# All pairs of a linear-attention kernel: k's sums and numerators in plain float32, two heads side by side in 64-column tiles, sums of k and denominators in four 32-column tiles

## The chip, the cores and the metric

The kernel runs on one core of a Trainium2 chip. TensorE (PE) multiplies matrices, VectorE (DVE) and ScalarE (ACT) work on tiles, GpSimd (POOL) makes one reduction, and SyncE (SP) starts the DMA transfers. The metric is the device time of one launch in microseconds (us), the median of several runs. The profiled execution is one more run, with its own time.

## The reference

The inputs are `q`, `k`, `v` of 8 batches, 8 heads, 576 positions and 64 numbers a head, `w_phi` (64 x 128) and three weights of a gated layer. Cut to what matters:

```
proj = x @ w_phi                                  # for q and for k: 576 x 128 a head
proj = proj - max(abs(proj), axis=-1)
phi  = concat(exp(proj), exp(-proj))              # 576 x 256
kv   = phi(k).T @ v                               # 256 x 64 a head
z    = phi(k).sum(over positions)                 # 256
num  = phi(q) @ kv ;  den = phi(q) @ z + 1e-6
x    = num / den, heads side by side              # 4608 tokens x 512
out  = ((x @ w_a) * (x @ w_b)) @ w_out            # 512 -> 1536 -> 512
```

All of it is float32.

## The kernel before, in words

**Products.** TensorE reads float32 in two ways here. A tile of type `F32` is multiplied as plain float32, where one matmul of the program shows as two records in the trace. A tile of type `F32R` is a rounded form that takes one record, and a float32 value is kept as two of these, a high part and a low part (`split`, lines 154 to 157: a cast, and a subtraction that finds the low part). The product of two split values is three matmuls (`products`, lines 108 to 112): high by high, high by low, low by high.

**Attention** goes by pairs of heads: 8 batches with 4 pairs, 32 pairs in all, which the text numbers 0 to 31. For a pair, `k_load` brings in k and v, `features` (lines 216 to 246) projects k in chunks of 128 positions, finds the maximum, subtracts it and takes the two exponentials. `kv_add` (lines 275 to 289) multiplies a chunk's features with v and adds into the PSUM tile `kvps`; v carries a 65th column of ones, so row 65 of the result is z. There are four full chunks (two to a `k_chunks`) and 64 positions left over, which two pairs share in one tile (`rest_chunk`, `rest_add`). `k_finish` (lines 295 to 314) copies `kvps` out, transposes it on TensorE into `pt`, and copies that to `kvh`. `kvps` and `pt` share one PSUM bank from batch 1 on (`spare`, line 293), so a pair's `kvps` waits until the readers of the `pt` before it are done. `q_project` projects q for both heads. `q_side` (lines 342 to 375) takes the maximum over partitions on GpSimd, subtracts, takes the exponentials and multiplies with `kvh`, for numerator and denominator in one, 65 rows of `pn`. `reciprocals` turns the denominators into factors.

**Which pairs are split.** The first pairs are plain float32: k's projections and q's up to pair 4, the products of `kv_add` up to pair 6 (`PLAIN_KV = 7`), the numerators up to pair 4 (`PLAIN_NUM = 5`). These five have a form of their own (`numerators`, lines 377 to 406): two heads write to rows 0 to 63 and 64 to 127 of one `pn`, each with 64 columns of weights, and the denominators go to four strips of 32 rows of `pd`. All later pairs are split: `keh`, `kel` (features of k), `vaug`, `vl` (v), `kvh`, `kvl` and `qeh`, `qel` (features of q).

**The gated layer** takes 512 tokens a block (`moe_block`, lines 618 to 671) for the first third of the 1536 columns, all in split form, while attention is still going; two later passes follow with another algorithm. `attention_steps` (lines 418 to 455) writes the stages of the pairs to turns, five turns a pair for the first seven and then four. In each turn the main loop (lines 1029 to 1040) lets `PACE` steps of the gated layer go (0.6 until turn 18, then 0.62). The order in which all this is written sets priorities; a scheduler with a model of the chip makes the final order of each engine's queue, and each engine then works through its queue in order. The places that the prediction speaks of are `kv_add`, `k_finish`, the end of `q_side`, `numerators`, and the matmuls of lines 645 and 666, the gated layer's.

## Time and profile before

| | |
|---|---|
| median of 3 runs | 1240.53 us (1240.15 to 1241.73) |
| profiled execution | 1247.55 us, span 1245.8 us |
| PE busy | 1200.6 us, 96% of the span |
| DVE busy | 1033.0 us, 83% |
| ACT busy | 696.2 us, 56% |
| POOL busy | 151.5 us, 12% |

The span is what the profiler saw from first to last instruction. A record of a matmul has a modelled end: matmuls overlap in the pipeline, so the time from one start to the next is what a matmul costs, and a busy PE can hold short gaps. POOL works until about 590 us, which is where attention ends. What follows is the rest of the first pass, and from about 700 us the later passes, which the change does not touch. In rows, `128*65` after the names is rows and columns of the weights, and `128x256` is the operand that streams past them.

### The profile page before, as it was taken

Reading aid. Unit: us, or ns where it says so; the run is one execution under the profiler, and the core shown is the slowest. Engines: PE = TensorE matmul, PEld = TensorE weight load, DVE = VectorE, ACT = ScalarE, POOL = GpSimd, SP = SyncE. Lnnn points to the kernel's source line nnn. Section 1 sums busy time; section 2 is a strip of 40 time slices with the busy share of each in tenths; the row PEclk is TensorE's granted clock in tenths of the full one; section 3 lists DMA queues with packets and bytes.
Section 4 is the critical chain, followed back from the end, with each engine's and each line's share of the span. In section 5 each row is a group of like instructions: output and inputs, shape, how many; then the busy total and the mean of one; then the engine's idle time right before and its main releaser. Section 6 shows DMA issues by size and latency. Waiting matters only on the chain.

```text
span 1245.8 us, 18250 instructions
## 1 busy us (share of the span) xinstructions
PE 1200.6 (96%) x6425; PEld 977.0 (78%) x6425; DVE 1033.0 (83%) x1742; ACT 696.2 (56%) x1317; POOL 151.5 (12%) x68
## 2 busy tenths in 40 slices
PE   7898999999999999999899999999999999999998
PEld 4456878778888878888678888888888888887887
DVE  6999988989989899796398865888888688888686
ACT  5667768778777777677244443444434243434332
POOL 2233132222231322212000000000000000000000
PEclk9999999999999999999999999999999999999999
DMA  6664443443443543323373331657489724242412
GB/s 198 186 199 119 109 136 94 118 150 102 129 127 93 145 110 113 110 80 91 93 254 102 110 97 56 211 178 241 150 279 395 262 60 153 68 149 70 129 67 86
DMA packets 125360, 174.86 MB, mean 140 GB/s; under 512 B 34571, under 2 KB 63647, under 8 KB 125269
## 3 DMA queue, kind: packets, MB, share of 16 engines
q1 hardware_dynamic: 125268, 173.71, 45.0%
q8 instruction: 50, 0.82, 0.3%
q14 instruction: 42, 0.34, 0.1%
HBM read 115.10 MB, written 58.56 MB: 139 GB/s over the span
## 4 chain that ended last, share of the span: by engine, by line
PE 47%; DVE 14%; DMA 7%; issue 2%; ACT 2%; SPq 1%; DVEq 0%; ACTq 0%
PE pba L740 6%; PE po L952 6%; PE paa L740 6%; PE po L666 4%; PE pa L645 3%; PE poa L845 3%; PE pac L740 3%; PE pb L645 3%; PE pbc L740 3%; PE kvps L282 2%; PE pn L371 2%; PE pab L740 2%; PE pbb L740 2%; DMA rb<-rec 2%; DMA x<-xnorm 1%
## 5 line engine op out<-in xcount | busy, mean ns | idle before, releaser
L348 POOL PARTITION_ALL_REDUCE mb<-p x64 | 151.4, 2393 | 433.4 <-ACT p L339 363.8
L157 DVE TENSOR_TENSOR qel<-qe,qeh 128x1152 fp32r<-128x1152 f32 x54 | 74.6, 1381 | 7.4 <-ACT qeh L150 7.4
L238 ACT ACTIVATE ke<-kd 128x512 f32<-128x512 f32 x64 | 40.5, 634 | 65.8 <-DVE kd L230 65.5
L645 PE MATMUL pb<-xh,w_b_h 128*128 128x512 f32 x144 | 59.4, 412 | 7.1 <-DVE h L650 5.5
L352 ACT ACTIVATE qe<-p 128x576 f32<-128x576 f32 x64 | 44.0, 687 | 37.6 <-DVE p L349 35.6
L157 DVE TENSOR_TENSOR kel<-ke,keh 128x1024 fp32r<-128x1024 f32 x50 | 62.1, 1242 | 3.2 <-ACT keh L150 3.1
L282 PE MATMUL kvps<-keh,vaug 128*65 128x256 f32 x200 | 56.3, 281 | 7.2 <-DVE kvl L312 7.2
L150 ACT CAST qeh<-qe 128x1152 fp32r<-128x1152 f32 x54 | 62.8, 1163 | 0.0
L666 PE MATMUL po<-hh,w_o_h 128*128 128x512 f32 x144 | 58.5, 412 | 1.9 <-DVE h L650 1.9
L645 PE MATMUL pa<-xh,w_a_h 128*128 128x512 f32 x144 | 57.9, 402 | 1.5 <-DVE xh L152 1.4
L602 DVE TENSOR_TENSOR x<-x,rb 128x512 f32<-128x512 f32 x36 | 31.9, 887 | 33.1 <-DMA rb<-rec 31.0
L666 PE MATMUL po<-hl,w_o_h 128*128 128x512 f32 x144 | 58.4, 405 | 0.3 <-DVE hl L157 0.3
L645 PE MATMUL pb<-xl,w_b_h 128*128 128x512 f32 x144 | 58.3, 405 | 0.0
L645 PE MATMUL pb<-xh,w_b_l 128*128 128x512 f32 x144 | 58.2, 404 | 0.0
L645 PE MATMUL pa<-xl,w_a_h 128*128 128x512 f32 x144 | 57.5, 399 | 0.5 <-DVE xl L157 0.5
L645 PE MATMUL pa<-xh,w_a_l 128*128 128x512 f32 x144 | 57.8, 401 | 0.0
L666 PE MATMUL po<-hh,w_o_l 128*128 128x512 f32 x144 | 57.6, 400 | 0.0
L952 PE MATMUL po<-hl,w_o_h 128*128 128x512 f32 x144 | 56.4, 392 | 0.2
L952 PE MATMUL po<-hh,w_o_l 128*128 128x512 f32 x144 | 56.1, 389 | 0.0
L282 PE MATMUL kvps<-keh,vl 128*64 128x256 f32 x200 | 55.9, 279 | 0.0
L282 PE MATMUL kvps<-kel,vaug 128*65 128x256 f32 x200 | 55.8, 279 | 0.0
L150 ACT CAST keh<-ke 128x1024 fp32r<-128x1024 f32 x50 | 52.5, 1051 | 1.8 <-PE kvps L282 1.5
(343 smaller groups left out, 3838.9 us busy)
## 6 DMA issues: line engine op xcount, KB each, us to landing
x<-xnorm SPq DMA_DIRECT2D x32, 512.0 KB
o<-part SPq DMA_DIRECT2D x61, 256.0 KB
q<-in_qT SPq DMA_DIRECT2D x32, 288.0 KB
xnorm<-x SPq DMA_DIRECT2D x36, 256.0 KB
part<-o SPq DMA_DIRECT2D x18, 512.0 KB
part<-o SPq DMA_DIRECT2D x36, 256.0 KB
k<-in_km SPq DMA_DIRECT2D x32, 256.0 KB
v<-in_vm SPq DMA_DIRECT2D x32, 256.0 KB
```

The lines of the kernel that those rows point to most:

```text
L150: eng.copy(dst, src)
L157: eng_lo.tensor_tensor(lo, src, hi, op=ALU.subtract)
L238: nc.scalar.activation(e[:, :, 0, :], d, AF.Exp)
L282: nc.tensor.matmul(st["kv_ps", b, pr][:width, j], v_[:, j, :width], e_[:, j], start=(left == NFULL and j == 0 and n_ == 0), stop=(left == ...
L348: nc.gpsimd.partition_all_reduce(mb, p32, P, bass_isa.ReduceOp.absmax)
L352: nc.scalar.activation(e[:, 0], p32, AF.Exp)
L602: nc.vector.tensor_tensor(x32, x32, rb, op=ALU.mult)
L645: nc.tensor.matmul(acc, w[:, cc * P : (cc + 1) * P], x, start=(k == 0), stop=(k == 3 * NCC - 1))
L666: nc.tensor.matmul(acc, w[:, cc * P : (cc + 1) * P], h, start=(k == 0), stop=(k == 3 * NFS[p] - 1))
L740: nc.tensor.matmul(accs[to][i], w_, x_, skip_group_check=True, **at)
L845: nc.tensor.matmul(accs[to][m], w_, x_, skip_group_check=True, **flags)
L952: nc.tensor.matmul(acc[key], w[:, cc * P : (cc + 1) * P], h[:, tok], skip_group_check=True, **n_)
```

## The change

All pairs now use the plain form for the sums of k and for the numerators; the projections stay as they were (plain up to pair 4, split after).

* `kv_add` takes the chunks of a `k_chunks` together. For each, the two heads' products with v go to rows 0 to 63 and 64 to 127 of the first half of `kvps` (64 columns of weights each, plain float32). z no longer comes from a column of ones in v: a weight tile `ones` (32 columns) multiplies each chunk and head, into four strips of 32 rows of the second half of `kvps`. For the 64 positions left over it is the same with two products and two strips.
* `k_finish` makes two transposes of 128 columns instead of four of 65, and two small products with `pick`, which adds the strips up to the two z. `kvh` stays float32, and `kvl` is gone.
* `q_side` ends with the exponentials; `numerators` does what it did for the first five pairs, for all.
* The casts and subtractions for v, for the features of k and of q, and for `kvh` are gone, and the tiles for them. Their room goes to more buffers for the plain features (`qe` 4, `ke2` 4) and for v (3), and the decoding of the weights has tiles of its own (`w`) instead of sharing `kel2`.
* A pair's two `q_side` start two turns apart instead of three, and the numerators of both heads stand at turn 12 of a pair; before, they stood at 10 and 13 (split) or 13 (plain). `PACE` is 0.68 instead of 0.62.

```diff
-Q_TURNS, Q_STEP, QB, PB, Q32 = (4, 6, 10), 3, 1, 2, 2
+Q_TURNS, Q_STEP, NUM_TURN, QB, PB, Q32 = (4, 6), 2, 12, 1, 2, 2
-PACE0, PACE, PACE0_UNTIL = 0.6, 0.62, 18
-PLAIN_K, PLAIN_Q, PLAIN_KV, PLAIN_NUM = 5, 5, 7, 5
+PACE0, PACE, PACE0_UNTIL = 0.6, 0.68, 18
+PLAIN_K, PLAIN_Q = 5, 5
...
+        ones = a1.tile([P, P // 4], F32, name="ones")
+        nc.vector.memset(ones, 1.0)
+        pick = a1.tile([P, 2], F32, name="pick")
+        nc.vector.memset(pick, 0.0)
+        for g in range(4):
+            nc.vector.memset(pick[g * P // 4 : g * P // 4 + 1, g % 2 : g % 2 + 1], 1.0)
...
-        if i >= PLAIN_KV:
-            va = vaug[pr % 2]
-            vl = a1.tile([P, NFULL, 2, D + 1], F32R, tag="vl", bufs=2, name=f"vl_{u}")
-            split(va[:, :, :, :D], vl[:, :, :, :D], v32, engine("v_hi", b), engine("v_lo", b))
-            st["v", b, pr] = (va, vl)
...
+        e = a2.tile([P, 2 * n, 2, F], F32, tag=f"ke{n}", bufs=(2, 4)[n - 1], name=f"ke_{u}")
         nc.scalar.activation(e[:, :, 0, :], d, AF.Exp)
         nc.scalar.activation(e[:, :, 1, :], d, AF.Exp, scale=-1.0)
-        es = (e,)
-        if not plain:
-            eh = a2.tile(shape, F32R, tag=f"keh{n}", bufs=n, name=f"keh_{u}")
-            el = a2.tile(shape, F32R, tag=f"kel{n}", bufs=n, name=f"kel_{u}")
-            split(eh, el, e, engine("ke_hi", i // NPAIR), nc.vector)
-            es = (eh, el)
-        yield es
+        yield e
...
-    def kv_add(b, pr, vs, es, st):
-
-        left = st["kv_left", b, pr] = st["kv_left", b, pr] - 1
-        for j in range(2):
-            parts = products(vs, es)
-            for n_, (v_, e_) in enumerate(parts):
-                width = D if n_ == 2 else D + 1
-                nc.tensor.matmul(
-                    st["kv_ps", b, pr][:width, j],
-                    v_[:, j, :width],
-                    e_[:, j],
-                    start=(left == NFULL and j == 0 and n_ == 0),
-                    stop=(left == 0 and n_ == len(parts) - 1),
-                    skip_group_check=True,
-                )
+    def kv_add(b, pr, chunks, consts, st, rows=slice(0, P)):
+
+        ones = consts[6]
+        kv = st["kv_ps", b, pr]
+        first = st["kv_left", b, pr] == NFULL + 1
+        left = st["kv_left", b, pr] = st["kv_left", b, pr] - len(chunks)
+        for c, (v, e) in enumerate(chunks):
+            at = dict(start=(first and c == 0), stop=(left == 0), skip_group_check=True)
+            for j in range(2):
+                nc.tensor.matmul(kv[j * D : (j + 1) * D, 0], v[:, j], e[:, j], **at)
+        q = P // 4
+        for c, (v, e) in enumerate(chunks):
+            for j in range(2):
+                g = 2 * c + j
+                to = kv[g * q : (g + 1) * q, 1]
+                at = dict(start=False, stop=(left == 0), skip_group_check=True)
+                nc.tensor.matmul(to, ones[rows], e[:, j], tile_position=(rows.start, g * q), **at)
...
-        kvT = a2.tile([P, 4, F], F32, tag="kb", bufs=1, name=f"kvT_{u}")
-        nc.scalar.copy(kvT[: D + 1], st["kv_ps", b, pr][: D + 1].rearrange("p j (s f) -> p (j s) f", s=2))
+        kvT = a2.tile([P, 2, 2, F], F32, tag="kb", bufs=1, name=f"kvT_{u}")
+        nc.scalar.copy(kvT, st["kv_ps", b, pr].rearrange("p k (s f) -> p k s f", s=2))
...
-        for g in range(4):
-            nc.tensor.transpose(pt[:, g, : D + 1], kvT[: D + 1, g, :], ident[: D + 1, : D + 1])
...
+        for s in range(2):
+            nc.tensor.transpose(pt[:, s, :P], kvT[:, 0, s], ident)
+        for s in range(2):
+            nc.tensor.matmul(pt[:, s, P : P + 2], kvT[:, 1, s], consts[7], skip_group_check=True)
+        kvh = a2.tile([P, 2, P + 2], F32, tag="kvh", name=f"kvh_{u}")
+        nc.scalar.copy(kvh, pt[:, :, : P + 2])
...
-            split(eh, el, e, engine("qe_hi", b), nc.vector)
...
-        for i in range(2):
-            tok = slice(i * HALF, (i + 1) * HALF)
-            pn = ps.tile([P, 512], F32, tag="att", name=f"pn_{u}_{i}")
-            for n_, (s, kv_, e_) in enumerate(parts):
-                at = dict(start=(n_ == 0), stop=(n_ == len(parts) - 1))
-                nc.tensor.matmul(pn[: D + 1, :HALF], kv_[:, 2 * j + s, :], e_[:, s, tok], **at)
-            nc.scalar.copy(xn[: D + 1, tok], pn[: D + 1, :HALF])
-        nc.sync.dma_start(xun[b][h * D : (h + 1) * D], xn[:D])
-        nc.sync.dma_start(den[b][h : h + 1], xn[D : D + 1])
```

Three places in the order of the queues show what moves. The first is TensorE at the sums of k, pair 1 of batch 4: `kvps` is the sum, `keh`, `kel`, `vaug`, `vl` the split operands, `po` the gated layer's. Before, from the end of a `po` through the first of two chunks:

```order
L666 MATMUL po_0_2_0_3869<-hl_0_2_2_3691,w_0_2_o_h_641 128x512
L666 MATMUL po_0_2_0_3869<-hh_0_2_2_3690,w_0_2_o_l_642 128x512
L282 MATMUL kvps_4_1_3848<-keh_4_1_0_3714,vaug1_131 65x256
L282 MATMUL kvps_4_1_3848<-kel_4_1_0_3715,vaug1_131 65x256
L282 MATMUL kvps_4_1_3848<-keh_4_1_0_3714,vl_4_1_3449 64x256
```

The three `kvps` rows then stand three times more. With the change, the end of the k projection `pk`, the first two chunks, the end of the `po` behind them, the other two chunks and the rest, with `ke` the plain features and `v32`, `rv32` the plain v:

```order
L200 MATMUL pk_4_1_r_3438<-wkh_110,rkl_4_1_3296 128x256
L247 MATMUL kvps_4_1_3408<-ke_4_1_0_3266,v32_4_1_2853 64x256 x4
L254 MATMUL kvps_4_1_3408<-ke_4_1_0_3266,ones_129 32x256 x4
...
L604 MATMUL po_0_2_1_3449<-hh_0_2_3_3332,w_0_3_o_l_716 128x512
L247 MATMUL kvps_4_1_3408<-ke_4_1_2_3417,v32_4_1_2853 64x256 x4
L254 MATMUL kvps_4_1_3408<-ke_4_1_2_3417,ones_129 32x256 x4
L247 MATMUL kvps_4_1_3408<-ke_4_0_r_3195,rv32_4_0_2678 64x256 x2
L254 MATMUL kvps_4_1_3408<-ke_4_0_r_3195,ones_129 32x256 x2
```

Twelve matmuls of a `k_chunks` are now eight, and the width of the weights alternates between 64, 32 and the 128 of the neighbours. The second place is TensorE at the numerators `pn` and denominators `pd` of the same pair. Before, for the first of its two heads (`qeh_4_2`), whose partner stands elsewhere in the queue:

```order
L371 MATMUL pn_4_2_0_4114<-qeh_4_2_3905,kvh_4_1_4019 65x288 x2
L371 MATMUL pn_4_2_0_4114<-qel_4_2_3906,kvh_4_1_4019 65x288 x2
L371 MATMUL pn_4_2_0_4114<-qeh_4_2_3905,kvl_4_1_4021 65x288 x2
L371 MATMUL pn_4_2_1_4122<-qeh_4_2_3905,kvh_4_1_4019 65x288 x2
L371 MATMUL pn_4_2_1_4122<-qel_4_2_3906,kvh_4_1_4019 65x288 x2
L371 MATMUL pn_4_2_1_4122<-qeh_4_2_3905,kvl_4_1_4021 65x288 x2
```

With the change, for both heads (`qe_4_2` and `qe_4_3`), from the second half of the tokens on, between a small product `pt` with `pick` and the next k projection:

```order
L272 MATMUL pt_4_2_3720<-pick_131,kvT_4_2_3650 128x2
L329 MATMUL pn_4_1_1_3696<-qe_4_2_3420,kvh_4_1_3566 64x288
L329 MATMUL pn_4_1_1_3696<-qe_4_3_3568,kvh_4_1_3566 64x288
...
L339 MATMUL pd_4_1_3702<-qe_4_2_3420,kvh_4_1_3566 32x288 x2
L339 MATMUL pd_4_1_3702<-qe_4_3_3568,kvh_4_1_3566 32x288 x2
...
L200 MATMUL pk_5_0_0_3734<-wkh_110,kh_5_0_3637 128x256
```

Both heads stand together, and the denominators are matmuls of their own. The third place is ScalarE between two exponentials of k (`ke`) of the same pair. Before:

```order
L238 ACTIVATE ke_4_1_0_3711<-kd_4_1_0_3506 128x4x128
L239 ACTIVATE ke_4_1_0_3711<-kd_4_1_0_3506 128x4x128
...
L150 CAST keh_4_1_0_3714<-ke_4_1_0_3711 128x1024
L372 COPY xn_3_6_3614<-pn_3_6_0_3615 65x288
L372 COPY xn_3_6_3614<-pn_3_6_1_3623 65x288
L150 CAST qeh_4_0_3642<-qe_4_0_3639 128x1152
L150 CAST vaug0_129<-v32_4_2_3454 128x8x64
```

With the change:

```order
L207 ACTIVATE ke_4_1_0_3266<-kd_4_1_0_3133 128x4x128
L208 ACTIVATE ke_4_1_0_3266<-kd_4_1_0_3133 128x4x128
L312 ACTIVATE qe_4_1_3374<-p32_4_0_1_3060 128x576
L313 ACTIVATE qe_4_1_3374<-p32_4_0_1_3060 128x576
L147 CAST hh_0_2_1_3179<-h32_0_2_1_3176 128x512
L207 ACTIVATE ke_4_1_2_3417<-kd_4_1_2_3241 128x4x128
```

The casts `keh`, `qeh` and `vaug` are gone from between the exponentials. On VectorE the subtractions that went with them, `kel`, `qel`, `vl` and `kvl`, are gone in the same way.

More of the change, by code (lines that the diff above doesn't have):

```diff
@@ L137, in attention_consts @@
         nc.sync.dma_start(ident, diagonal[: P * P].rearrange("(p n) -> p n", n=P))
-        vaug = []
-        for i in range(2):
-            t = a1.tile([P, NFULL, 2, D + 1], F32R, name=f"vaug{i}")
-            nc.vector.memset(t[:, :, :, D : D + 1].bitcast(F32), 1.0)
-            vaug.append(t)
-        return w2, wh, wl, wk32, (wkh, wkl), ident, vaug
+        ones = a1.tile([P, P // 4], F32, name="ones")
[4 more added lines that the diff above has]
+            nc.vector.memset(pick[g * P // 4 : g * P // 4 + 1, g % 2 : g % 2 + 1], 1.0)
+        return w2, wh, wl, wk32, (wkh, wkl), ident, ones, pick
     def engine(step, b):
@@ L197, in rest_load @@
         nc.sync.dma_start(k32, kr[b, g])
-        v32 = a1.tile([P, 2, D + 1], F32, tag="rv32", name=f"rv32_{u}")
-        nc.vector.memset(v32[:, :, D : D + 1], 1.0)
-        nc.sync.dma_start(v32[:, :, :D], vr[b, g])
+        v32 = a1.tile([P, 2, D], F32, tag="rv32", bufs=2, name=f"rv32_{u}")
+        nc.sync.dma_start(v32, vr[b, g])
+        st["rv", b, g] = v32
         yield
@@ L206, in rest_load @@
             st["rk", b, g] = (kh, kl)
-        yield
-        st["rv", b, g] = (v32,)
-        if i >= PLAIN_KV:
-            vh = a1.tile([P, 2, D + 1], F32R, tag="rvh", name=f"rvh_{u}")
-            vl = a1.tile([P, 2, D + 1], F32R, tag="rvl", name=f"rvl_{u}")
-            split(vh, vl, v32, engine("v_hi", b), engine("v_lo", b))
-            st["rv", b, g] = (vh, vl)
         yield
@@ L252, in k_chunks @@
         yield next(gen)
-        es = next(gen)
+        e = next(gen)
         yield
@@ L258, in k_chunks @@
             st["kv_left", b, pr] = NFULL + 1
-        for c in range(2):
-            kv_add(b, pr, [v_[:, c0 + c] for v_ in st["v", b, pr]], [e_[:, 2 * c : 2 * c + 2] for e_ in es], st)
+        v = st["v", b, pr]
+        kv_add(b, pr, [(v[:, c0 + c], e[:, 2 * c : 2 * c + 2]) for c in range(2)], consts, st)
         yield
@@ L298, in k_finish @@
         assert st["kv_left", b, pr] == 0
-        kvT = a2.tile([P, 4, F], F32, tag="kb", bufs=1, name=f"kvT_{u}")
-        nc.scalar.copy(kvT[: D + 1], st["kv_ps", b, pr][: D + 1].rearrange("p j (s f) -> p (j s) f", s=2))
+        kvT = a2.tile([P, 2, 2, F], F32, tag="kb", bufs=1, name=f"kvT_{u}")
+        nc.scalar.copy(kvT, st["kv_ps", b, pr].rearrange("p k (s f) -> p k s f", s=2))
         yield
         pool, tag, bufs = spare(b, ps)
-        pt = pool.tile([P, 4, P], F32, tag=tag, bufs=bufs, name=f"pt_{u}")
-        for g in range(4):
-            nc.tensor.transpose(pt[:, g, : D + 1], kvT[: D + 1, g, :], ident[: D + 1, : D + 1])
-        plain = b * NPAIR + pr < PLAIN_NUM
-        kvh = a2.tile([P, 4, D + 1], F32 if plain else F32R, tag="kvh", name=f"kvh_{u}")
-        nc.scalar.copy(kvh, pt[:, :, : D + 1])
-        st["kv", b, pr] = (kvh,)
-        if not plain:
-            kvl = a2.tile([P, 4, D + 1], F32R, tag="kvl", name=f"kvl_{u}")
-            nc.vector.tensor_tensor(kvl, pt[:, :, : D + 1], kvh, op=ALU.subtract)
-            st["kv", b, pr] = (kvh, kvl)
+        pt = pool.tile([P, 2, 2 * P], F32, tag=tag, bufs=bufs, name=f"pt_{u}")
+        for s in range(2):
[4 more added lines that the diff above has]
+        nc.scalar.copy(kvh, pt[:, :, : P + 2])
+        st["kv", b, pr] = kvh
         yield
@@ L342, in q_side @@
     def q_side(b, pr, j, a1, a2, ps, consts, st):
[L343 to L345 removed]
+        u = f"{b}_{2 * pr + j}"
         p32 = st["p", b, pr][j]
@@ L350, in q_side @@
         yield
[L351 removed]
+        e = a2.tile([P, 2, S], F32, tag="qe", bufs=4, name=f"qe_{u}")
         nc.scalar.activation(e[:, 0], p32, AF.Exp)
         nc.scalar.activation(e[:, 1], p32, AF.Exp, scale=-1.0)
[L354 to L374 removed]
+        st["qe", b, pr, j] = e
         yield
     def numerators(b, pr, a1, a2, ps, consts, st):
[L379 to L380 removed]
         u = f"{b}_{pr}"
[L382 removed]
+        kv, es = st["kv", b, pr], [st["qe", b, pr, j] for j in range(2)]
         toks = [slice(i * HALF, (i + 1) * HALF) for i in range(2)]
@@ L387, in numerators @@
             for s in range(2):
-                for j, e in enumerate((e0, e1)):
+                for j, e in enumerate(es):
                     at = dict(start=(s == 0), stop=(s == 1), skip_group_check=True)
-                    nc.tensor.matmul(pn[j * D : (j + 1) * D, :HALF], kv[:, 2 * j + s, :D], e[:, s, tok], **at)
+                    rows = slice(j * D, (j + 1) * D)
+                    nc.tensor.matmul(pn[rows, :HALF], kv[:, s, rows], e[:, s, tok], **at)
             nc.scalar.copy(xn[:, tok], pn[:, :HALF])
@@ L577, in stage @@
                 return xpool.tile(shape, dt, tag="o", bufs=2, name=name)
-            return pool.tile([P, 2 * DM], dt, tag="kel2", bufs=2, name=name)
+            return pool.tile([P, 2 * DM], dt, tag="w", bufs=2, name=name)
         return stage
```

67 lines of the change are left out of this document (14 added, 53 removed).

## The prediction

> **What bounds the kernel now.** I read the shares of busy time first, then a table by stage, then the timeline of single matmuls, and last the waits. The page and the stage table (columns: window, its length, busy time of PE, PEld, DVE, ACT, POOL, granted clock, DMA share, GB/s):
>
> ```profile
> PE 1200.6 (96%) x6425; PEld 977.0 (78%) x6425; DVE 1033.0 (83%) x1742; ACT 696.2 (56%) x1317; POOL 151.5 (12%) x68
> ```
>
> ```profile
> 31.00:124.00 93.00, 83.76 (x490) 50.70 (x487) 88.14 (x160) 66.70 (x140) 29.36 (x12) 0.98 0.56 169
> 124.00:590.00 466.00, 452.18 (x2846) 380.36 (x2845) 410.63 (x628) 350.85 (x671) 113.30 (x48) 1.00 0.40 114
> 590.00:651.00 61.00, 55.44 (x244) 43.41 (x243) 38.26 (x81) 24.09 (x50) 0.00 (x0) 0.94 0.56 170
> 651.00:1246.00 595.00, 585.16 (x2755) 487.79 (x2753) 474.57 (x826) 238.71 (x426) 0.00 (x0) 1.00 0.46 151
> ```
>
> PE is the bound in every stage but the second, where DVE is busy 88 of 93 us and PE waits for it. In 124 to 590, where the split pairs run, DVE is at 88% and PE at 97%: PE is the bound and DVE makes it wait now and then. So the change has to be judged in PE time first, and the relief of DVE and ACT counts only as far as PE waits for them. A matmul's true price is the distance between starts, since its modelled end overlaps the next:
>
> ```profile
> 302.40 0.28 PE L282 MATMUL kvps<-keh,vaug 128*65 128x256 f32 x1
> ...
> 303.68 0.28 PE L282 MATMUL kvps<-keh,vl 128*64 128x256 f32 x1
> 303.89 0.40 PE L337 MATMUL pq<-qh,wh 64*128 64x288 f32 x2
> 304.13 0.29 PE L337 MATMUL pq<-ql,wh 64*128 64x288 f32 x2
> ...
> 304.65 0.29 PE L337 MATMUL pq<-qh,wl 64*128 64x288 f32 x2
> 304.87 0.50 PE L645 MATMUL pa<-xh,w_a_h 128*128 128x512 f32 x1
> 305.21 0.39 PE L645 MATMUL pa<-xl,w_a_h 128*128 128x512 f32 x1
> 305.44 0.40 PE L645 MATMUL pa<-xh,w_a_l 128*128 128x512 f32 x1
> ...
> 308.24 0.41 PE L305 MATMUL pt<-ident,kvT 65*128 65x65 f32 x4
> 308.46 0.37 PE L226 MATMUL pk<-wkl,kh 128*128 128x256 f32 x1
> ...
> 311.60 0.42 PE L371 MATMUL pn<-qeh,kvh 128*65 128x288 f32 x2
> ...
> 313.17 0.40 PE L666 MATMUL po<-hh,w_o_h 128*128 128x512 f32 x1
> ```
>
> Eleven steps of split `kvps` take 1.28 us, **0.117 us** each. The twelve split `pn` of one head take 1.57 us, **0.131** each. Four transposes take 0.22, 0.06 each. And there is a price that no group shows: where the shape of the weights changes from 128 rows to 64 (`kvps` to `pq`) the step is 0.21 instead of 0.117, and the first `pq` takes 0.24 instead of 0.13; back to 128 rows 0.22 instead of 0.13, and the first `pa` 0.34 instead of 0.23. **One change of shape costs about 0.09 us, and 0.11 more for the first weights of 128 columns, 0.20 in all.**
>
> The plain forms that the change spreads are in the trace too, in the first pairs:
>
> ```profile
> 11.86 1.94 PE L282 MATMUL kvps<-ke,v 128*65 128x256 f32 x8
> 13.73 0.75 PE L337 MATMUL pq<-q,w 64*128 64x288 f32 x2
> ...
> 64.16 1.18 PE L399 MATMUL pd<-qe,kvh 128*32 128x288 f32 x16 [0.21 <-ACT xn L391]
> 65.26 0.75 PE L337 MATMUL pq<-q,w 64*128 64x288 f32 x2
> ...
> 73.22 0.28 PE L226 MATMUL pk<-wkh,kl 128*128 128x256 f32 x1
> 73.42 2.16 PE L390 MATMUL pn<-qe,kvh 128*64 128x288 f32 x16
> 75.52 1.16 PE L399 MATMUL pd<-qe,kvh 128*32 128x288 f32 x10
> ```
>
> A plain product shows as two records. Four plain `kvps`, one after the other, take 1.87 us to the next start, of which 0.14 is the change of shape: 0.43 each, more than three split ones (0.35). Eight plain `pn` with two heads side by side take 2.10: without 0.14 for the changes that is 0.49 for two of them, so **two heads in 64-column tiles really run at once**. Eight `pd` in four strips take 1.10, without 0.11 again 0.49 for four. For 256 elements instead of 288 that is 0.43 for two products, or four strips. Entering `pn` from `pk` costs 0.20 instead of 0.117, the 0.09 again. For narrower weights the second part of a change is smaller: 0.05 for 64 columns and 0.02 for 32, worked out from these sums.
>
> **The change part by part, on PE.** How many of each there are is counted in the order.
>
> Sums of k: before, 744 split matmuls at 0.117 and 72 plain at 0.43, 118.1 us. After, 128 times two products at once, 64 sets of four strips, and for the rest 32 times two products and 32 times two strips, each 0.43, with a few that the order tears apart: 112.3. Numerators: before 648 at 0.131 and five plain pairs, 99.9. After, six times 0.485 a pair, and some `pn` alone where gated-layer matmuls stand between the heads: 96.2. Transposes: before 128 at 0.06, 7.8. After, 64 of twice the width, for which I take 0.07, and 128 records of the small products with `pick` at 0.06 (nothing in the trace is as short; between 0.03 and 0.12): 12.3. The q projections keep their number, but the order sets two heads side by side more often: 35.3 to 29.8. Together 261.1 to 250.6, **10.5 us less**.
>
> Changes of shape: the order has 202 before and **432** after (into 64, into 32, into the next wide shape, where before a split sum or numerator stood between wide neighbours at no charge). At 0.20, 0.14 and 0.11 by the width they go into, 39.0 become 66.4, **27.4 more**. PE's own work grows by **17 us**. Bounds: 10, if only the 0.09 is paid for each of the 230, and 27, if none of the 10.5 comes in.
>
> On this the Trainium skill has a rule, in "TensorEngine Tiling (Array Packing)", Key Properties: changing the tiling mode, not just the tile, drains the engine. It speaks against this change, and the trace agrees that such a change costs. If the drain were the whole modelled tail of a record (0.28 less 0.117, 0.16) instead of the 0.09 of the rows, the 230 would cost 16 us more; the rows decide for 0.09.
>
> **What DVE and ACT give back.** In 124 to 590 the groups that go (count, busy us, mean ns, idle before):
>
> ```profile
> L157 DVE TENSOR_TENSOR qel<-qe,qeh 128x1152 fp32r<-128x1152 f32 x49 | 67.1, 1370 | 7.4 <-ACT qeh L150 7.4
> L157 DVE TENSOR_TENSOR kel<-ke,keh 128x1024 fp32r<-128x1024 f32 x49 | 60.9, 1243 | 3.2 <-ACT keh L150 3.1
> L157 DVE TENSOR_TENSOR vl<-v,vaug 128x512 fp32r<-128x512 f32 x23 | 19.8, 860 | 0.0
> L312 DVE TENSOR_TENSOR kvl<-pt,kvh 128x260 fp32r<-128x260 f32 x24 | 10.0, 416 | 0.0
> L150 ACT CAST qeh<-qe 128x1152 fp32r<-128x1152 f32 x48 | 55.8, 1162 | 0.0
> L150 ACT CAST keh<-ke 128x1024 fp32r<-128x1024 f32 x48 | 50.4, 1050 | 1.8 <-PE kvps L282 1.5
> L150 ACT CAST vaug<-v 128x512 fp32r<-128x512 f32 x23 | 14.2, 617 | 1.8 <-PE kvps L282 1.8
> ```
>
> DVE loses 158 of 411 us and falls to 54%, ACT 120 of 351, to 50%. All of it lies beside PE work, so it is worth only PE's waits. These are, by the waits of PE and one place in the timeline:
>
> ```profile
> PE kvps L282 <- DVE kvl L312: 7.2, 9, 2.1
> PE pb L645 <- DVE h L650: 5.5, 3, 2.9
> PE po L666 <- DVE h L650: 1.9, 1, 1.9
> ```
>
> ```profile
> 615.63 0.80 PE L645 MATMUL pb<-xh,w_b_h 128*128 128x512 f32 x1 [2.93 <-DVE h L650]
> 616.22 0.63 PE L645 MATMUL pb<-xl,w_b_h 128*128 128x512 f32 x1
> ```
>
> By the stage table PE is idle 9.2, 13.8 and 5.6 us in the three stages up to 651. A wait hides 0.16 us in the modelled tail before it, and behind a long one the clock is low for a while (the step at 616 is 0.43 instead of 0.23; the table's 0.98 and 0.94 are 1.9 and 3.7 us). From start to start, without the changes of shape, I count 13, 26 and 10 us in these stages, **49 in all**. What returns: in the split stage 15 of 26, since `kvps` no longer waits for `kvl`, and half-empty queues bring `h` and the features sooner; in 31 to 124 only 4 of 13, since plain pairs and the decoding of weights still fill DVE there; after 590 4 of 10, since both orders end attention with the same two and a half blocks of the gated layer or a little less. **23 in all.** Bounds: 7 (the one wait that disappears by name), and 42.
>
> `PACE` and the new turns only reorder work that PE must do anyway; their price is in the waits. A pair's four output transfers become two, and POOL is busy 24% in 124 to 590; PE waits for neither in that stage.
>
> **The sum:** 17 less 23 is **6 us less** against the profiled execution's 1247.55. That one lies 7.0 above the median 1240.53, so the median would be 1234.5; I say 1235.
>
> **The rivals.** (1) *Nearly all waits go.* With DVE and ACT at half, PE could run as in 651 to 1246, where it is idle 9.8 of 595 us, end and transitions included. For it: ample slack on every other engine. Against it: in that stage DVE is at 80% and still gives few waits, so load alone does not make them, and 31 to 124 stays full. 17 less 41: 1217. (2) *The changes of shape win.* PE pays its 17 us surely, at every pair, while the waits are those of chains that the change leaves: `pb` waits for `h`, which needs `pa` copied by ACT and multiplied by DVE with two banks between; `kvps` now waits for the copy `kvh` on ACT in place of `kvl`. It decides as soon as fewer than 17 of the 49 come back. With the 7 of the named wait alone: 10 more, 1250. For it: the rows of 0.20 are firm; against it: 8 us of the listed waits are at DVE's `h`, behind a queue that is emptied by a third. (3) *The heads do not run at once in the sums* (the change doesn't do what it says): 160 double steps and the strips one after the other, 0.43 each, add about 70 and 90 us, some 1390. Against it stand the `pn` and `pd` rows, of the same form.
>
> **How the numbers follow.** Forecast, between 15 less and 2 more: 0.50. Nearly all waits go: 0.17. Shapes win: 0.28. No overlap: 0.05. A measurement of this kernel tells about 0.2%, 2.5 us, from no change. Faster by more: 0.37 of the forecast and all of (1), 0.54. Within: 0.13 of the forecast and 0.04 of (2), 0.17. Slower: 0.24 and 0.05, 0.29. The range leaves out (3) and the ends of (1) and (2): 1219 to 1253.
>
> **What would show it.** Right: plain `kvps` groups of about 1.0 (two chunks' products) and 0.54 us (strips), steps of 0.20 around them, DVE at 55% in the attention stage, PE's listed waits below half, the later passes unchanged. Wrong: changes of shape dearer or cheaper than 0.20, or new waits of `kvps`, `pn` or `pt` on ACT's copies of the size of the old ones.

## The result: 1.3% slower

| | before | changed |
|---|---|---|
| median of four runs each | 1241.13 us (1240.15 to 1245.71) | 1258.39 us (1253.47 to 1260.68) |
| profiled execution | 1247.55 us | 1259.20 us |
| first matmul of the later passes starts at | 702.8 us | 711.8 us |

The ratio is 1.0126, with a 95% interval of 1.0087 to 1.0166. The forecast was 1235 us; the sign is wrong and the time lies outside the range. Between the two profiled executions there are 11.7 us: 9.0 before the later passes begin, 2.9 in them, and 0.2 less at the end.

First the shares of busy time and the table by stage of the changed kernel (columns as in the table of before: window, its length, PE, PEld, DVE, ACT, POOL, granted clock, DMA share, GB/s):

```profile
PE 1227.7 (98%) x7097; PEld 894.3 (71%) x7097; DVE 879.7 (70%) x1543; ACT 571.3 (45%) x1137; POOL 145.6 (12%) x68
```

```profile
31.00:124.00 93.00, 85.70 (x595) 48.11 (x594) 84.68 (x148) 59.82 (x130) 28.21 (x13) 0.94 0.57 178
124.00:590.00 466.00, 464.66 (x3228) 297.67 (x3226) 259.09 (x440) 228.83 (x490) 103.85 (x46) 1.00 0.36 110
590.00:651.00 61.00, 58.64 (x339) 40.60 (x332) 28.47 (x57) 21.53 (x46) 4.30 (x2) 1.00 0.46 151
651.00:1246.00 595.00, 589.46 (x2747) 489.95 (x2746) 478.99 (x833) 242.62 (x435) 0.00 (x0) 1.00 0.45 152
```

DVE fell from 410.6 to 259.1 us in 124 to 590 and ACT from 350.9 to 228.8, much as predicted. PE is now busy 464.66 of 466 us there: it waits for nothing, and yet it takes longer. POOL's work, which ends with attention, still shows 4.30 us after 590, where before it shows none. The list of PE's waits says the same (engine, line, what it waited for, us in all, times, longest; ahead of these rows stands the first load of k, 5.6 us, which before has too):

```profile
PE pt L270 <- ACT kvT L265: 3.5, 2, 2.8
...
PE kvps L247 <- ACT kvh L274: 1.7, 1, 1.7
```

The 7.2 us of `kvps` behind `kvl` are gone, and of the 5.5 us of `pb` behind `h` 0.7 are left. From its first matmul to the start of the later passes PE is idle for 13.7 us instead of 29.9, and busy for 692.6 instead of 667.2 (the view by windows, 5.56 to 711.81 and 5.71 to 702.77). The added time is therefore inside PE's own work. The timeline of PE where one pair's sums of k end (start, length, line, what, columns as before):

```profile
324.86 0.39 PE L604 MATMUL po<-hh,w_o_l 128*128 128x512 f32 x1
325.18 1.08 PE L247 MATMUL kvps<-ke,v 128*64 128x256 f32 x8
326.19 0.64 PE L254 MATMUL kvps<-ke,ones 128*32 128x256 f32 x8
326.76 0.65 PE L247 MATMUL kvps<-ke_r,rv 64*64 64x256 f32 x4
327.34 0.62 PE L254 MATMUL kvps<-ke_r,ones 64*32 64x256 f32 x4
327.89 0.40 PE L299 MATMUL pq<-qh,wh 64*128 64x288 f32 x2
...
328.88 0.50 PE L604 MATMUL po<-hh,w_o_h 128*128 128x512 f32 x1
329.21 0.40 PE L604 MATMUL po<-hl,w_o_h 128*128 128x512 f32 x1
```

From 324.86 to 329.21 are 4.35 us. The products in it, at the prediction's prices, are 0.23 of `po`, 0.86 for four products of two heads, 0.43 each for the strips, the products left over and their strips, 0.79 for twelve `pq`, and 0.23 of `po`: 3.40. The other 0.95 us are six changes of shape, 0.16 each, without a single wait in it. Before, such a place had two, into the 64 rows of the products left over and `pq`, and out of them. Each step is the one predicted: 0.32 instead of 0.23 ahead of `kvps`, 1.01 and 0.57 for its groups, 0.24 for the first `pq`, 0.33 for the first `po`.

Where numerators and transposes stand:

```profile
312.06 2.16 PE L329 MATMUL pn<-qe,kvh 128*64 128x288 f32 x16
314.15 1.18 PE L339 MATMUL pd<-qe,kvh 128*32 128x288 f32 x16
315.26 0.44 PE L270 MATMUL pt<-ident,kvT 128*128 128x128 f32 x2
315.54 0.51 PE L272 MATMUL pt<-pick,kvT 128*128 128x2 f32 x4
315.90 0.36 PE L200 MATMUL pk<-wkh,kh 128*128 128x256 f32 x1
316.10 0.28 PE L200 MATMUL pk<-wkl,kh 128*128 128x256 f32 x1
```

`pn` takes 2.09 and `pd` 1.11, as priced: the heads do run at once. But the two transposes and the four records with `pick` take 0.64 us, and the `pk` behind them 0.20 instead of 0.117. The first step behind transposes is as dear before the change: the `pk` behind the four of before, too, takes 0.21.

```profile
308.46 0.37 PE L226 MATMUL pk<-wkl,kh 128*128 128x256 f32 x1
308.67 0.28 PE L226 MATMUL pk<-wkh,kl 128*128 128x256 f32 x1
```

**Where the 9 us come from.** I took PE's time from the first matmul to the start of the later passes, start to start, in three parts: the products at the prediction's prices (0.117 and 0.131 for split ones, 0.43 and 0.49 for plain, 0.06 for a transpose or a record of it, 0.233 for one of 512 columns); the changes of shape counted in the trace at the prediction's prices (0.09, and 0.11, 0.05 or 0.02 for the first weights, with weights of 65 columns counted like 64); and all that is left, which is waits, the slow clock behind them, and products that are dearer than priced.

| us | products | changes of shape (number) | left | sum |
|---|---|---|---|---|
| before | 615.2 | 36.3 (202) | 45.6 | 697.1 |
| changed | 604.4 | 67.1 (432) | 34.7 | 706.2 |
| difference | -10.8 | +30.8 | -10.9 | +9.1 |

The experiments take these three apart.

### The profile page after: what moved, and what is told of

It reads as the page before. It is cut to its first block, busy times and chain, and to the rows that moved or that the text cites. A ratio compares the mean times of both kernels' runs of the same rounds, so it can differ in the third digit from the quotient of the medians.

```text
span 1257.4 us, 19136 instructions
## 1 busy us (share of the span) xinstructions
PE 1227.7 (98%) x7097; PEld 894.3 (71%) x7097; DVE 879.7 (70%) x1543; ACT 571.3 (45%) x1137; POOL 145.6 (12%) x68
## 4 chain that ended last, share of the span: by engine, by line
PE 81%; DVE 11%; DMA 5%; ACT 1%; issue 1%; SPq 0%; ACTq 0%; DVEq 0%
PE po L890 8%; PE pa L583 7%; PE po L604 7%; PE pb L583 7%; PE pba L678 7%; PE paa L678 7%; PE kvps L247 5%; PE pn L329 5%; PE kvps L254 3%; PE pac L678 3%; PE pbc L678 3%; PE pk L200 3%; PE poa L783 3%; PE pd L339 2%; PE pq L299 2%; PE pab L678 2%
## 5 line engine op out<-in xcount | busy, mean ns | idle before, releaser
L308 POOL PARTITION_ALL_REDUCE mb<-p x64 | 145.4, 2310 | 449.9 <-ACT p L301 405.9
L309 DVE TENSOR_TENSOR p<-p,mb 128x576 f32<-128x576 f32 x64 | 64.9, 1015 | 20.7 <-POOL mb L308 20.7
L540 DVE TENSOR_TENSOR x<-x,rb 128x512 f32<-128x512 f32 x36 | 26.6, 741 | 73.0 <-DMA rb<-rec 67.1
L329 PE MATMUL pn<-qe,kvh 128*64 128x288 f32 x512 | 75.6, 415 | 0.0
L247 PE MATMUL kvps<-ke,v 128*64 128x256 f32 x512 | 71.2, 400 | 1.7 <-ACT kvh L274 1.7
L203 DVE TENSOR_REDUCE m<-pk 128x4 f32<-128x512 f32 x64 | 43.7, 683 | 37.4 <-PE pk L200 37.4
L329 PEld LDWEIGHTS pn<-qe,kvh 128*64 128x64 f32 x512 | 34.3, 136 | 28.7 <-issue 9.7
L147 ACT CAST hh<-h 128x512 fp32r<-128x512 f32 x36 | 22.3, 619 | 69.4 <-DVE h L588 69.3
L247 PEld LDWEIGHTS kvps<-ke,v 128*64 128x64 f32 x512 | 31.6, 138 | 30.2 <-issue 15.0
```

The lines of the kernel that those rows point to most:

```text
L203: nc.vector.tensor_reduce(out=m[:, : 2 * n], in_=p, op=ALU.max, axis=AX.X, apply_absolute_value=True)
L247: nc.tensor.matmul(kv[j * D : (j + 1) * D, 0], v[:, j], e[:, j], **at)
L308: nc.gpsimd.partition_all_reduce(mb, p32, P, bass_isa.ReduceOp.absmax)
L309: engine("q_sub", b).tensor_tensor(p32, p32, mb, op=ALU.subtract)
L329: nc.tensor.matmul(pn[rows, :HALF], kv[:, s, rows], e[:, s, tok], **at)
```

## The experiments

The theory after the result: the changes of shape cost 31 us by their price, the relief of DVE and ACT returns about 20 us of waits, and the saved products are partly eaten by dearer ones. The rivals: the relief returned little; the new turns and the pace of the gated layer did it; the plain numerators or the plain sums do harm by themselves. All results stand in one table at the end of this section.

**The kernel before, once more.** A second profile, no edit.

> The kernel before, unchanged, for a second profile. The profile that the prediction was summed against lies 7 us above the median, the one of the change 1 us above its own. If the 7 us were waits of that one execution, this profile has fewer waits of TensorE up to 650 us than its 46, some 40, and ends near 1241 to 1243. If they lie around the span: the same waits.

It took 1244.69 us, 2.9 less than the first profile. Up to the later passes its left part is 42.8 instead of 45.6, and the products, the changes of shape and the later passes (538.2 to 538.1) are the same. So the first profile, against which the prediction made its sum, held some 3 us that belong to that execution alone, and what a version returns is 3 us less when it is counted from the second profile.

**Relief alone.** The split kernel with the same matmuls, without the casts and subtractions that make low parts. It leaves out the low parts of the features, of v and of `kvh`: the high part is multiplied in their place, so the result is another.

```diff
-            split(eh, el, e, engine("ke_hi", i // NPAIR), nc.vector)
-            es = (eh, el)
+            es = (e, e)
...
-            st["v", b, pr] = (va, vl)
+            st["v", b, pr] = (va, va)
...
-            st["kv", b, pr] = (kvh, kvl)
+            st["kv", b, pr] = (kvh, kvh)
```

> The kernel before, with the low parts of the features of k and q, of v and of kvh left out (the exponentials write the rounded form themselves, and the high part is multiplied in the place of the low one, so the result lacks those terms). TensorE multiplies as much as before, VectorE and ScalarE lose the same work as in the change. The order has 160 changes of shape instead of 202, 8 us less by the prices of the rows. If relief of VectorE and ScalarE gives back the 23 us of the prediction: 1241 less 8 less 23, about 1210. If it gives back only 5 to 11, as the two traces suggest: 1222 to 1228. If nothing: 1233.

1218.97 us, ratio 0.9802 (0.9782 to 0.9822). Its stage row (columns as above) shows that DVE falls by 161 us, as against 152 in the change, and ACT by 92 as against 122, since the cast of v and the copies `xn` of single heads stay:

```profile
124.00:590.00 466.00, 457.42 (x2924) 392.55 (x2923) 249.32 (x474) 258.63 (x570) 105.47 (x48) 1.00 0.40 116
```

The left part falls from 45.6 to 25.6, by 20 us, and 42 changes of shape fewer give 8.2 more by their price, because the scheduler, with other times of readiness, laid the products out differently. Counted from the second profile of before, the left part falls by 17; the medians, 25.5 us apart, leave some 15 beside the 8.2 and the 1.9 us by which the products are cheaper. So the relief is worth 15 to 20 us, less than the 23 of the prediction but most of it, and the 1210 expected for all 23 did not come. PE is idle for 16.7 us up to the later passes, where the changed kernel has 13.7 and before has 29.9 and 28.4 in its two profiles: the change got at least as much idle time back as the relief alone. The first rival falls.

**More changes of shape, nothing else.** The changed kernel with each set of `pd` strips right behind its half of `pn`.

```diff
             nc.scalar.copy(xn[:, tok], pn[:, :HALF])
+            for g in range(4):
+                j, h = divmod(g, 2)
+                at = dict(start=(i == 0), stop=(i == 1), skip_group_check=True)
+                z = kv[:, i, P + j : P + j + 1].broadcast_to([P, q])
+                to = pd[g * q : (g + 1) * q, :HALF]
+                nc.tensor.matmul(to, z, es[j][:, i, toks[h]], tile_position=(0, g * q), **at)
-        for s in range(2):
-            for g in range(4):
...
```

> The changed kernel, with each half of the denominators right behind each half of the numerators: the same matmuls, but 483 changes of shape instead of 432. If each change into 64 or 32 columns costs the 0.12 to 0.14 us of the rows, 6 us more than the change: about 1264. If the changes are not what makes it slow: 1258.

The timeline of the piece that differs:

```profile
313.50 1.19 PE L331 MATMUL pn<-qe,kvh 128*64 128x288 f32 x8
314.62 0.69 PE L338 MATMUL pd<-qe,kvh 128*32 128x288 f32 x8
315.25 1.19 PE L331 MATMUL pn<-qe,kvh 128*64 128x288 f32 x8
316.37 0.69 PE L338 MATMUL pd<-qe,kvh 128*32 128x288 f32 x8
316.99 0.44 PE L270 MATMUL pt<-ident,kvT 128*128 128x128 f32 x2
```

The pair takes 3.49 us where the changed kernel takes 3.20 (312.06 to 315.26 above): two more changes, 0.145 each, with prices of 0.14 and 0.11 predicted. With 483 changes in all the median is 1261.6, ratio 1.0146 (1.0130 to 1.0162): above the changed kernel by 0.2%, which is inside both intervals, while in the profiles the later passes begin 4.0 us later, of 6.5 that the 51 changes cost by price.

**Fewer changes of shape, the same products.** In *grouped* all ten sums of a pair stand together and all ten strips behind them; the 64 positions left over take 128 rows, the other 64 filled with zeros, and all pairs add them at turn 7 (before, at 6 or 7). In *joined* the `pn` of the pair before stands ahead of the sums and its `pd` behind the strips, so that 64-column work meets 64-column work: the two lines `next(before, None)` are joined's alone, and `before` there is the pair before's `numerators`, which so leave turn 12; the reciprocals stand a turn later.

```diff
-        kv_add(b, pr, [(v[:, c0 + c], e[:, 2 * c : 2 * c + 2]) for c in range(2)], consts, st)
+        st.setdefault(("chunks", b, pr), []).extend(
+            (v[:, c0 + c], e[:, 2 * c : 2 * c + 2], consts[6]) for c in range(2)
+        )
...
-        kv_add(b, pr, [(st["rv", b, pr // 2][rows], st["re", b, pr // 2][rows])], consts, st, rows)
+        chunks = st["chunks", b, pr] + [(st["rv", b, pr], st["re", b, pr // 2], consts[8][pr % 2][0])]
+        next(before, None)
+        kv_add(b, pr, chunks, consts, st)
+        next(before, None)
```

> The changed kernel, with all ten products of a pair's sums together and then its ten strips, and the 64 left-over positions as a full chunk with zeros in v and in the ones of the other pair, so that they have the shape of the others. The same matmul time, but 303 changes of shape instead of 432, 17 us less by the prices of the rows: about 1241. If the changes are not the cause: 1258. If holding the sums back to one place brings waits that are as long: 1250 or more.

> As with all sums of a pair together, and the numerators of the pair before ahead of them and its denominators behind them, so that 64 columns stand by 64 and 32 by 32: 206 changes of shape instead of 432, 33 us less than the change by the prices of the rows: about 1226, below the kernel before. If the changes are not the cause: 1258. If the longer stretch without the gated layer makes the other engines late: 1235 to 1245.

Grouped: 303 changes, 1247.04 us, ratio 1.0031 (1.0018 to 1.0045). Joined: 206 changes, as few as before, 1243.39 us, ratio 0.9989 (0.9968 to 1.0010). One pair's visit in the timeline of joined:

```profile
331.68 2.16 PE L343 MATMUL pn<-qe,kvh 128*64 128x288 f32 x16
333.67 1.90 PE L261 MATMUL kvps<-ke,v 128*64 128x256 f32 x16
335.39 0.60 PE L261 MATMUL kvps<-ke_r,rvz 128*64 128x256 f32 x4
335.93 1.07 PE L268 MATMUL kvps<-ke,ones 128*32 128x256 f32 x16
...
337.09 1.29 PE L354 MATMUL pd<-qe,kvh 128*32 128x288 f32 x14
338.31 0.40 PE L313 MATMUL pq<-qh,wh 64*128 64x288 f32 x2
```

`pn` now takes 1.99 to the next start instead of 2.09, and eight products of `kvps` 1.72, which is 0.43 for two and nothing for a change; from 331.68 to 338.31 there are three changes. The whole loss of the change is gone, with all its products kept. What speaks against the rivals of pace and turns is that grouped and joined have the pace of the change and turns near it. But it isn't faster than before: of 32.9 us less in changes of shape 18 arrive at the start of the later passes, since waits grow as PE gets faster: its idle time up to there is 22.1 us against 13.7 in the change. The time is in the range expected for late engines, not at the 1226 of the price alone. One of these waits in joined's timeline:

```profile
608.39 0.79 PE L601 MATMUL pb<-xh,w_b_h 128*128 128x512 f32 x1 [3.74 <-DVE h L606]
608.98 0.63 PE L601 MATMUL pb<-xl,w_b_h 128*128 128x512 f32 x1
...
613.67 0.41 PE L622 MATMUL po<-hh,w_o_h 128*128 128x512 f32 x1
```

**The pace.** The changed kernel with the pace of before (*pace62*), and joined with a faster one, 0.74 in the same place (*joined_fast*).

```diff
-PACE0, PACE, PACE0_UNTIL = 0.6, 0.68, 18
+PACE0, PACE, PACE0_UNTIL = 0.6, 0.62, 18
```

> The change with the gated layer's pace of before (0.62 for 0.68): 419 changes of shape for 432. If the changes of shape are the cause and the pace is none, 13 fewer of them give 1 us: 1255 to 1260. Rival (the pace of 0.68 delays the attention's end and so the later passes): back by 5 us or more, 1253 or less, with the end of attention earlier by as much and the later passes starting earlier.

> The joined version (all sums of a pair at one place, with the numerators of the pair before around them) with a pace of 0.74 for 0.68; 294 changes of shape as counted in the order, for 292. In joined PE waits 3.7 us for h near 605 and then runs on a low clock, because attention has ended and the gated layer's chain is alone. If that tail is what keeps joined at the time of before, a later end of attention covers it: 1236 to 1240. Rival (the waits belong to the joined order wherever the pace puts them): 1242 to 1246.

With 0.62 the changed kernel takes 1256.67 us, ratio 1.0092 (1.0064 to 1.0121), and its later passes begin 2.6 us earlier, with 2.3 us fewer in changes of shape. So the pace has at most a small part in the loss: the 5 us or more of the rival did not come back. Joined with 0.74 takes 1241.34 us, ratio 0.9979 (0.9961 to 0.9998). The wait of 3.74 us near 605 is gone from its list of waits, and the later passes begin at 690.1 instead of 693.7; in that profile they then last 543.8 us where joined's last 539.2, nearly all of it between 800 and 900 us, where PE once waits 1.8 us for `hh` and the clock is 0.98 on average instead of 1.00. It is the fastest version that computes everything, by 0.2% against before, which is just at what a measurement of this kernel can tell; against joined nothing is settled, since the intervals overlap, and the time lies between the two ranges expected. (The 294 and 292 changes of the expectation are no count of the table: up to the later passes the traces show 208 and 206.)

**The two halves apart.** *num_only* is the kernel before with plain numerators for all pairs, by one constant. *num_buf* is that with four buffers for the plain `qe` and a buffer of its own for `dn`, as the change has them. *sums_only* has the plain sums in the grouped form, and numerators, turns and pace of before; to split `kvh` it needs two copies and two subtractions a pair, where before needs one of each. The first two lines of the diff are those of both num_only and num_buf, the others of num_buf alone; sums_only takes its `kv_add` from grouped, as shown above.

```diff
-PLAIN_K, PLAIN_Q, PLAIN_KV, PLAIN_NUM = 5, 5, 7, 5
+PLAIN_K, PLAIN_Q, PLAIN_KV, PLAIN_NUM = 5, 5, 7, 32
...
-        e = a2.tile([P, 2, S], F32, tag="qeh" if plain else "qe", bufs=2, name=f"qe_{u}")
+        e = a2.tile([P, 2, S], F32, tag="qe", bufs=4, name=f"qe_{u}")
...
-        dn = a2.tile([P, 4 * F], F32, tag="kd", bufs=2, name=f"dn_{u}")[:, :HALF]
+        dn = a2.tile([P, HALF], F32, tag="dn", bufs=1, name=f"dn_{u}")
```

> The kernel before, with the plain numerators for all pairs and the sums split as they were. The order has 318 changes of shape instead of 202, 17 us more by the prices of the rows; TensorE's products are 4 us less, and the overlap of the left-over products with the q projection stays. VectorE loses the subtractions for q's features (67 us in 124 to 590), ScalarE the casts (56). By my theory that PE work and returned waits add up, with about half of the 20 us of waits coming back: 1241 plus 13 less 10, about 1244. If relief of VectorE alone set the time: below 1235. If the changes of shape came with more than their price: above 1250.

> The plain sums of a pair all together, with the left-over positions padded with zeros, and the numerators split as before, with the turns and the pace of before. The order has 211 changes of shape, as many as before (202) and 4 us cheaper; the products are 6 us less, but the transposes with the small products cost 13 more and the overlap of the left-over products with the q projection goes (5). VectorE loses some 100 us, ScalarE some 70. By my theory: PE 8 us more, and 12 of the 20 us of waits back: about 1237. If the plain sums cost as the whole change does: above 1250.

> The kernel before with only the numerators of all pairs plain, as in num_only, but with the buffers that the change gives them: four for the plain features of q and one of its own for the copied denominators. 252 changes of shape against 202 before, 318 in num_only and 432 in the change. My theory (the changes of shape are what makes the change slow, and the stall of num_only came from its two buffers): the products of the numerators fall by 6, some 50 changes of shape at 0.09 to 0.12 add 5 to 6, and of the relief's 20 us of waits about half returns, since qel and qeh go and kel, keh, vl, kvl stay: 8 to 12 less than the kernel before, 1232 to 1237. Rival (plain numerators do harm of their own, by the wait for both heads, whatever the buffers): 1250 or more, and waits of PE on ACT's qe as in num_only. Second rival (the waits come back only where the work on k's side goes): 1241 to 1246.

num_only: 1384.45 us, ratio 1.1137 (1.1107 to 1.1167), far outside what was expected. PE is at 399 of 466 us and the clock at 0.92, and ACT's waits show one reason: both `qe` buffers are held until `pd` of the pair has read them. The largest row is that of `ke` behind `kd`, 114.3 us where before has 65.5; the two `kd` buffers also hold the copied denominators `dn` here.

```profile
124.00:590.00 466.00, 398.99 (x2377) 291.09 (x2376) 264.23 (x436) 235.00 (x460) 77.04 (x35) 0.92 0.30 92
```

```profile
ACT ke L238 <- DVE kd L230: 114.3, 43, 7.2
...
ACT qe L352 <- PE pd L399: 48.6, 22, 5.6
```

With the buffers the time is 1247.11 us, ratio 1.0021 (1.0006 to 1.0036): the stall was the buffers'. Whether the four of `qe` or the one of `dn` ended it is not told apart, since num_buf has both. But my theory's 1232 to 1237 fell as well. The terms on PE came as expected (products 6.0 less, changes of shape 4.7 more); the waits did not come back: the left part is 43.3 for 45.6. DVE is busy 343.97 of 466 us, a sixth less than before, and PE still waits for it in the same measure, at another place (first row; before, the largest were `kvl` and `h`):

```profile
PE pk L226 <- DVE kd L230: 8.6, 3, 3.8
...
PE po L666 <- DVE h L650: 5.5, 1, 5.5
```

sums_only: 1244.78 us, ratio 1.0010 (0.9991 to 1.0028), with a left part of 50.9, where 1237 was expected. So each half alone is worth nothing and does little harm, and neither returns much of the waits, although each takes a part of the split work off DVE: PE's idle time up to the later passes is 27.9 us in num_buf and 25.6 in sums_only, against 29.9 and 28.4 before. Together, in relief and in the change, the halves return 15 to 20 us. That the waits come back only with the work on k's side, as the second rival of num_buf had it, does not fit either, since sums_only takes that work off. Why the gain comes only with both is not settled by these runs.

**The relief in another way.** The kernel before with the subtraction for `kel` on GpSimd, for the full chunks and for the positions left over.

```diff
-            split(eh, el, e, engine("ke_hi", i // NPAIR), nc.vector)
+            split(eh, el, e, engine("ke_hi", i // NPAIR), nc.gpsimd)
```

> The kernel before, with the low part of k's features (kel of the full chunks) found on GpSimd instead of VectorE. TensorE's work and its changes of shape are those of before. VectorE loses 61 us, GpSimd, busy 24% in the split stage, takes them on. If relief of VectorE is worth a share of the 20 us of waits without a price on TensorE: about 1233. If GpSimd is too slow, or late with the maxima for it, the sums wait for kel: above 1260.

1434.31 us, ratio 1.1532 (1.1498 to 1.1566). POOL's groups in 124 to 590 (count, busy, mean ns, idle before them):

```profile
L157 POOL TENSOR_TENSOR kel<-ke,keh 128x1024 fp32r<-128x1024 f32 x36 | 95.5, 2661 | 150.2 <-ACT p L339 35.2 <-issue 22.0 <-ACT keh L150 20.7
L348 POOL PARTITION_ALL_REDUCE mb<-p x35 | 76.6, 2224 | 121.7 <-issue 67.6 <-ACT xn L372 11.8 <-PE kvps L282 11.6
```

The subtraction takes 2661 ns there against 1243 on DVE, and POOL is idle for 67.6 and 22.0 us that no event explains ("issue") ahead of the two kinds of work, which alternate in one queue with the maximum that q needs. PE then waits for POOL's `kel`, 40.5 us over the run, and for that of the positions left over, 28.9. This is no cheap way to the relief.

**All of them.** Columns as in the table of the result; the ratio is that of the medians, and the start of the later passes is that of the profile. The products of the two joined versions are taken from grouped, which has the same; in alternate and pace62 groups that are torn apart are counted up to 2 us differently.

| | products | changes of shape | left | later passes start | ratio to before |
|---|---|---|---|---|---|
| before | 615.2 | 36.3 (202) | 45.6 | 702.8 | |
| before, again | 615.2 | 36.3 (202) | 42.8 | 700.0 | |
| changed | 604.4 | 67.1 (432) | 34.7 | 711.8 | 1.0126 |
| relief | 613.3 | 28.1 (160) | 25.6 | 672.7 | 0.9802 |
| alternate | 606.0 | 73.6 (483) | 30.6 | 715.8 | 1.0146 |
| pace62 | 602.7 | 64.8 (419) | 36.1 | 709.2 | 1.0092 |
| grouped | 604.3 | 49.9 (303) | 39.6 | 699.3 | 1.0031 |
| joined | 604 | 34.2 (206) | 50 | 693.7 | 0.9989 |
| joined, pace 0.74 | 604 | 34.5 (208) | 46 | 690.1 | 0.9979 |
| sums only | 610.5 | 35.6 (211) | 50.9 | 702.5 | 1.0010 |
| numerators, 4 buffers | 609.2 | 41.0 (252) | 43.3 | 699.3 | 1.0021 |
| numerators, 2 buffers | 605.4 | 52.7 (318) | 178.2 | 841.9 | 1.1137 |

From the changed kernel to grouped and joined, 17.2 and 32.9 us of changes of shape go, and the later passes begin 12.5 and 18.1 us earlier. Between 0.55 and 0.73 of the price arrives; most of the rest turns into waits.

## Why the prediction was wrong

**What held.** PE is the bound, and it was right to judge the change in PE time. The heads run at once, in `pn` and in the sums (rival 3 is out). The price of a change of shape held at every place that can be read: 0.09 on the last step ahead (0.32 for 0.23), 0.14 into 64 columns (1.01 for four products of 0.86, with the tail ahead of the strips), 0.24 for the first `pq`, 0.145 each in alternate. They were put at 27.4 us more and came to 30.8; most of the difference lies in the kernel before, where some 50 changes lead into weights of 65 columns. The first such step costs 0.05 beside its 0.117 (433.76 to 433.93 below), while the prediction's 39.0 for before has them at about 0.11. The products were put at 10.5 less, and by their prices came to 10.8 less. The Trainium skill, "TensorEngine Tiling (Array Packing)", Key Properties, has it that a change of tiling mode drains the engine; the steps agree that it costs, and put it at 0.09 and the first weights, not at the whole modelled tail that a strict reading would make it.

**The step that failed is "PE's own work grows by 17 us".** It grew by about 29. By the profile's own count PE's busy time grows by 25.4 us up to the later passes while its idle time falls by 16.2; 37 gaps become 13, and each that goes also uncovers the 0.16 us of modelled tail that it hid, some 4 us in all. By price -10.8 and +30.8 make 20. The 9 between 20 and 29 are products that cost more than the sum had them for, and they are why the change's left part fell by 10.9 only, though about 20 us of waits went from it. Three are seen in the rows. *The transposes and `pick`:* 0.64 us a pair, where 0.38 was taken with 0.11 for the first weights: 0.15 a pair, 5 us in 32 pairs. For `pick`, 0.06 a record was taken, with the remark "nothing in the trace is as short"; it is 0.09, above the 0.06 of a transpose of 65 columns. The Trainium skill's "TensorEngine Tiling (Array Packing)", Instruction Overhead, says that a matmul of one column takes as long as one of sixty; the trace agrees that two columns are not cheap. *An overlap that the change removed:* before, the split products of the 64 positions left over ran at once with the q projection where the two stood side by side, as the prediction did not notice. In the timeline of before:

```profile
433.76 0.33 PE L282 MATMUL kvps<-keh_r,rvh 64*65 64x256 f32 x1
433.93 0.28 PE L282 MATMUL kvps<-kel_r,rvh 64*65 64x256 f32 x1
434.05 0.28 PE L282 MATMUL kvps<-keh_r,rvl 64*64 64x256 f32 x1
434.05 0.40 PE L337 MATMUL pq<-qh,wh 64*128 64x288 f32 x1
...
434.28 0.28 PE L282 MATMUL kvps<-kel_r,rvh 64*65 64x256 f32 x1
434.29 0.29 PE L337 MATMUL pq<-ql,wh 64*128 64x288 f32 x1
```

Over the whole order that made the 64-row products some 3 us cheaper than their price. In the changed kernel the products left over have 64 columns and the `pq` behind them 128, and the two follow one another (327.34 to 328.13 above). *The strips* of the full chunks take 0.57 to 0.58 instead of 0.54, 2 us in 64 sets. These sum to some 10, a little more than the 9; the parts were read from single places and are not exact, and no run takes one of them alone.

**The waits came out a little below the forecast:** 15 to 20 us return, 23 were predicted, most of them in the split stage. PE's idle time by the stage tables falls in 31 to 124 from 9.2 to 7.3, in 124 to 590 from 13.8 to 1.3, and in 590 to 651 from 5.6 to 2.4, about 18 in all against the predicted 4, 15 and 4; the tails and the slow clock come on top of it.

**The later passes** were to stay as they are. In the changed kernel's profile they take 2.9 us more, with one wait of 1.4 us for `hh` in them and the slow clock behind it; in grouped they take 538.1 and in alternate 538.0, as before. So the changed work does not bring it; whether other executions of the changed kernel have it is not known.

**The base.** The prediction took the distance of 7.0 us between profile and median as something that the changed kernel would share. The changed kernel's profile lies 0.8 above its median. In the later comparisons the median of before was 1243.2 to 1244.5, so that 3 or 4 of the 7 were the three runs and some 3 the one execution. The corrected sum is 29 - 20 + 3 = 12 against the profile, where 11.7 was measured; the runs say 16 (1.26% of 1241), and the difference is this base.

**The rivals.** Rival 2, "The changes of shape win", named the right side and cause, with 1250. Its condition was not the one that decided: it asked that fewer than 17 us of waits return, and 15 to 20 did, which is about that bound; but against 29 us of own work even the full 23 would have left the kernel slower. The chance that it got, 0.28, followed from the 17 us, which had a range of 10 to 27 and came out above it. The upper bound let the saving of 10.5 fail to come in, but held no dearer `pick` (0.12 a record was named as its bound and then left out) and no product that ran for nothing beside others before.

## What to carry to other kernels

Where TensorE is the bound, read the steps from start to start at each place where the shape of the weights changes, count such places in the new order, and then lay the work out so that equal shapes meet: the same products cost 1.3% more or nothing, by their order alone. Relief of an engine beside the bound returns waits only up to what the bound waits for, and half of such a relief can return almost none of it. Before taking an operation off, look whether it runs at the same time as another; its price is then less than its duration.

## What the hardware showed that was not expected

* **Products of 64 rows beside products of other 64 rows** start within 0.02 us of each other (434.28 and 434.29 above) although they belong to different stages of the program and to different PSUM tiles; no line of the kernel asks for it.
* **Two columns cost almost what 128 do.** Where no change of shape stands ahead, as in joined, two plain transposes of 128 columns take 0.22 us, 0.11 each, and four records with two columns 0.36, 0.09 each.

```profile
326.70 0.38 PE L284 MATMUL pt<-ident,kvT 128*128 128x128 f32 x2
326.92 0.51 PE L286 MATMUL pt<-pick,kvT 128*128 128x2 f32 x4
327.28 0.36 PE L211 MATMUL pk<-wkh,kh 128*128 128x256 f32 x1
```

* **A wait costs its length and more:** in joined, behind 3.74 us of waiting, the steps of 512 columns are 0.43 instead of 0.233 from 608.98 to 613.67, eleven of them, 2.1 us on top.
* **Two kinds of work on GpSimd** leave it idle for 90 us in a stage of 466 (67.6 and 22.0 in the rows of *pool_low*), with no event to explain it. Before, where the maxima are alone, the named waits cover all but 11.5 of its 350.3 us of idle time there.
